# Memory-augmented attention kernel: adjacent score groups, halved second query/key chunk, memory sums in row tiles, last-token filler in column groups

## Chip, cores and metric

The kernel runs on one core of a Trainium2 chip. The metric is the device time of one execution in microseconds. Runs of the kernel before took 1844.02, 1857.45 and 1866.82 us; the median, 1857.45 us, is the time before. All profile times below come from one further execution under the profiler.

## What is computed

The program applies two block types twice: `x += A(ln(x))`, `x += B(ln(x))`, and both again. x is 2048 x 512 in bfloat16. B is a gated MLP with a spatial mix (w_sp, 2048 x 2048); the change does not touch it. A is attention with a memory that is carried from segment to segment, and only this part matters here:

```python
for s in range(n_seg):                       # 64 segments of 32 tokens
    h = concatenate([mem, xs])               # 8 memory rows + 32 tokens
    q, k, v = h @ Wq, h @ Wk, h @ Wv         # 32 heads of 128
    p = softmax(mask(q @ k.T * scale))
    o = (p @ v) @ Wo
    mem = o[:, :8]                           # feeds the next segment
    outs.append(o[:, 8:])
```

Segment s+1 cannot start its projections before segment s has produced its 8 new memory rows. So each attention block is a loop of 64 dependent segments, and there are 128 in the program.

## The kernel before, in words

**One segment.** `segment()` (L683) is a list of instructions in a fixed order: TensorE, VectorE and ScalarE run exactly in the order in which the program records them (`manual_schedule`, L511). GpSimd and the DMA queues are placed by the scheduler. The 40 rows of a segment are split. The 8 memory rows and the first 24 tokens are 32 rows that form `hA`, a 128x32 operand per quarter of the model dimension. The last 8 tokens of each of four segments are projected together for a block of 128 tokens (`hB`, 32 rows), one block ahead; that work is cut into small units and used as filler for TensorE (`b_units`, L570).

The segment's steps on TensorE, in order:

1. `qk(0)`, `qk(2)`, `qk(1)`, `qk(3)` (L762 to L767): q and k of the first and second half of the heads, called q0, k0, q1, k1 below. Each is one chunk of 16 matmuls, 32 columns of weights (hA) by 512 moving columns, in four column groups of the array, so that four run side by side (`mm_chunk`, L530). ScalarE casts the 128x512 result into `rows` (L701); VectorE turns it in 32x32 blocks into `QQ` or `KA` (L705).
2. `scores(0)` (L714): 16 pairs of keys and queries of the first half of the heads, in 64-column groups, into one bank of `psS`; then Exp on ScalarE (L726). `close(r)` (L728) multiplies by the mask on VectorE (L729).
3. `v_mm(0)`, a filler unit, `scores(1)`, `v_mm(1)`, a filler unit. The values are copied out by VectorE for half 0 (L776) and by ScalarE for half 1 (L782).
4. `psM` (L784 to L788): the softmax sums of the memory rows, four matmuls of the whole 128x128 array (`onesG` holds ones for one half of the partitions and zeros for the other), into the accumulator bank accB. ScalarE takes Ln and then Exp of -Ln (L802, L803): the reciprocal.
5. `pv(0)`, `pv(1)` (L739) and `psD`, the sums of the token rows (L793), in row tiles of 64. Then a filler unit.
6. VectorE multiplies the memory rows by the reciprocal (L807, one per half), and `wo_pass` (L595) multiplies all 32 heads by Wo: 128 matmuls of 128 columns in four column groups. Meanwhile ScalarE makes the reciprocals of the token rows (L805, L813), and `tok_out(0)` (L755) writes the first half's token rows: L757 for the first 24 tokens, L759 for the last 8.
7. `build_hA(s + 1)` (L651): copy_predicated puts the memory rows into the next segment's rows (L654), and a turn makes the next hA (L655). Then the output copy (L660), the fourth filler unit, `copies` (filler results, L586 on ScalarE), `tok_out(1)`, `turns` (filler results turned into the block's Q and K, L587 on VectorE), and `tail`.

**Filler.** Each segment has four filler points. In segments 1, 2 and 3 of a block they take `b_units`: two chunks of the next block's projection per segment, as 4, 4, 8 and 16 matmuls in column groups of 32; a result passes through the single bank accA. In the first segment of a block, from the fifth block on, they take `y_part` (L615): the last tokens' output projection, `wo_last` (L607), as 1, 1, 2 and 4 matmuls of the whole array, 512 columns each, summed by VectorE (L627). The first segments of the first four blocks and the last three segments of the last block have no filler. So the 128 segments are 90 with `b_units`, 24 with `y_part` and 14 with none.

**Pads.** `pads_of` (L671) splits some of the 512-column matmuls in two of 256, so that each segment has the same number of TensorE instructions, a whole number of pages of 256; `fills_of` (L663) gives the instructions of the four filler points. One matmul is two instructions, a weight load and the multiplication.

**PSUM.** Eight banks: accA and accB one each, `att` two (psS, later psD), `attO[0]` and `attO[1]` two each (values psV, later the PV results psO).

**Also running.** In some segments `spare1`, `spare2` and `tail` add row work to VectorE: residual add (L213), statistics (L138) and normalisation (L187, L223) of rows for the next stage.

Of the kernel before, what the change touches and what calls it, by code (L numbers as in the profile page):

```python
# [14 lines left out]
P = 128  # L15
# [463 lines left out]
def a_block(tc, c, rows, front, MV_in, RS_in, MV_out, RS_out, wqkv, Wo, S, first):  # L479
# [6 lines left out]
    with ExitStack() as ctx:  # L486
# [83 lines left out]
        def b_units(tb, early=False):  # L570
            bs = blk_state[tb]

            for k, j in enumerate((0, 2, 1, 3, 4, 5)):
                ps = (accA if k % 2 == 0 or not early else accB).tile([P, 512], F32, name="psb")
                for kts in (((0,), (1,), (2, 3)), ((0, 1, 2, 3),))[k % 2]:
                    mm_chunk(ps, lambda kt, cg: bs["hB"][:, kt, :],
                             lambda kt, cg: qk_rhs(j, kt, cg) if j < 4 else v_rhs(j - 4, kt, cg), kts)
                    if kts[-1] != KT - 1:
                        yield

                def out(j=j, ps=ps):
                    if j >= 4:
                        nc.scalar.copy(bs["VB"][:, j - 4].rearrange("p i e -> p (i e)"), ps[:])
                        return
                    r = rowp.tile([P, 512], BF16, name="rowsB", bufs=2)
                    nc.scalar.copy(r[:], ps[:])  # L586
# [17 lines left out]
        def store_last(G, eng):  # L604
            eng.dma_start(o_d[M + 512 * G:M + 512 * G + 512, :].rearrange("(j r) d -> j r d", r=32)[:, 24:32, :], yB.pop(G)[:])

        def wo_last(G, heads, pwB):  # L607

            for h in heads:
                n = h // 8 * 8 + 2 * (h % 4) + h // 4 % 2  # L610
                nc.tensor.matmul(pwB[:], lhsT=oBs[G][:, n, :], rhs=Wo_sb[:, h, :].rearrange("p (kt g el) -> p g kt el", kt=4, g=4),  # L611
                                 start=(h == heads[0]), stop=(h == heads[-1]))
                yield

        def y_part(G, q):  # L615

            pwB = accA.tile([P, DM], F32, name="pwB")
            for k, _ in enumerate(wo_last(G, range(8 * q, 8 * q + 8), pwB)):
# [12 lines left out]
            adds.append(out)  # L631
            yield
# [30 lines left out]
        def fills_of(s):  # L663

            if s < 0:
                return FILL_AHEAD[not first]
            if s % 4 == 0:
                return (2, 2, 4, 8) if s // 4 > 3 else (0, 0, 0, 0)
            return (8, 8, 16, 32) if s // 4 + 1 < NB else (0, 0, 0, 0)

        def pads_of(s):  # L671

            n = (3 * PE_PAGE - SEGMENT_PE - fills_of(s - 1)[3] - sum(fills_of(s)[:3]) + 1) // 2
            pads = dict.fromkeys(("q0", "k0", "q1", "k1", "v0", "v1"), 0)
            for chunk, most in (("v0", 16), ("k1", 16), ("v1", 16 if s % 4 == 0 else 8), ("q1", 12), ("k0", 8), ("q1", 16), ("v1", 16),
                                ("k0", 16), ("q0", 16)):
                k = min(n, most - pads[chunk])
                pads[chunk] += k
                n -= k
            assert n == 0  # L680
            return pads

        def segment(s, fill, spare1, spare2, tail):  # L683
# [20 lines left out]
            def qk_T(j, r):  # L704
                nc.vector.transpose(out=QQ[:, j % 2, :, 0:32] if j < 2 else KA[:, j % 2], in_=r[:])  # L705

            def v_mm(r, ps):
                mm_chunk(ps, lambda kt, cg: hA_cur[:, kt, :], lambda kt, cg: v_rhs(r, kt, cg), halved=pads[("v0", "v1")[r]])

# [4 lines left out]
            def scores(r):  # L714

                pS = psS[:, r, 0:448].rearrange("p (i c) -> p i c", i=4)
                for i in range(4):
                    for K, c0 in ((KA, 0), (KTB, 80)):
                        for g in range(2):
                            n = 4 * i + 2 * g  # L720
                            q = QQ[:, r, n:n + 2, :]
                            nc.tensor.matmul(pS[64 * g:64 * g + 64, i, c0:80 if K is KA else 112],  # L722
                                             lhsT=K[:, r, n:n + 2, :].rearrange("p h k -> p (h k)"),
                                             rhs=q if K is KA else ends(q),
                                             start=(i == 0 and K is KA), stop=True, tile_position=(0, 64 * g), skip_group_check=True)
                nc.scalar.activation(out=E[:, r], in_=pS, func=ACT.Exp, scale=scale)  # L726

            def close(r):  # L728
# [23 lines left out]
            def hview(t, r, lo, hi):  # L752
                return t.rearrange("p (b n) q -> p b n q", b=4)[:, 2 * r:2 * r + 2, :, lo:hi]

            def tok_out(r):  # L755
                Rr = Rt[:].rearrange("p g (r n q) -> p g r n q", r=2, n=8)[:, :, r]
                nc.vector.tensor_tensor(out=hview(uT_nxt[:], r, 8, 32), in0=oview(r, 8, 32),  # L757
                                        in1=Rr[:, :, :, 0:24], op=ALU.mult)
                nc.vector.tensor_tensor(out=hview(oB, r, 8 * (s % 16), 8 * (s % 16) + 8), in0=oview(r, 32, 40),  # L759
                                        in1=Rr[:, :, :, 24:32], op=ALU.mult)  # L760
# [24 lines left out]
            for g in range(2):  # L785
                o = psM[:, 128 * g:128 * g + 128]
                nc.tensor.matmul(o, lhsT=onesG[:, g, :], rhs=a_part(0, P, 0, 2, 0, 8), start=(g == 0), stop=True, skip_group_check=True)  # L787
                nc.tensor.matmul(o, lhsT=onesG[:, g, :], rhs=b_part(0, P, 0, 2, 0, 8), start=False, stop=True, skip_group_check=True)  # L788
            psO = [attO[r].tile([P, 2, 512], F32, name="psO") for r in range(2)]
            psD = att.tile([P, 2, 512], F32, name="psD")  # L790
            pv(0)
            pv(1)
            for part, q0, q1, c0 in ((a_part, 8, 40, 0), (b_part, 8, 16, 24)):  # L793
                for r in range(2):
                    for g in range(2):
                        o = psD[:, g, 256 * r:256 * r + 256].rearrange("p (n q) -> p n q", q=32)[:, :, c0:32]
                        nc.tensor.matmul(o, lhsT=ones[64 * g:64 * g + 64, :], rhs=part(64 * g, 64 * g + 64, r, r + 1, q0, q1),  # L797
                                         start=(part is a_part and r == 0), stop=True, skip_group_check=True)
# [3 lines left out]
            nc.scalar.activation(out=rm, in_=psM[:, 0:256], func=ACT.Ln)  # L802
            nc.scalar.activation(out=rm, in_=rm, func=ACT.Exp, scale=-1.0)  # L803
# [35 lines left out]
        for s in range(NSEG):  # L839
# [87 lines left out]
```

The softmax here doesn't subtract the row's maximum and nothing guards it: scores larger than these inputs give would overflow.

## Time and profile before

| what | value |
|---|---|
| median of 3 runs | 1857.45 us |
| profiled execution | 1850.3 us |
| its span, first to last instruction | 1848.6 us |
| granted TensorE clock, mean | 0.991 |
| first attention block, 52 to 773 us | 721 us; TensorE busy 706, VectorE 492, ScalarE 503 |
| first B block, 773 to 958 us | 185 us; TensorE busy 164 |
| second attention block, 958 to 1684 us | 726 us; TensorE busy 713, VectorE 486, ScalarE 503 |
| end, from 1684 us | 165 us |
| scores, matmuls (psS) | 4096, mean 184 to 208 ns each |
| psM, matmuls | 512, mean 219 and 223 ns |
| cast of a 128x512 chunk on ScalarE (L701) | 512 x 586 ns |
| turn of a 128x512 chunk on VectorE (L705) | 512 x 711 ns |
| Exp of the scores (L726) | 256 x 547 ns |
| mask product (L729) | 256 x 372 ns |
| Ln, Exp for the memory rows (L802, L803) | 128 x 385 ns, 128 x 417 ns |

A matmul's duration is from its issue to its end; matmuls are pipelined, so that successive ones start much closer together than they last. How much time a stretch costs is therefore read from starts, not from sums of durations.

### The profile page before, as it was taken

How to read it: one execution, taken by the hardware profiler on the slowest of the kernel's cores; microseconds unless marked ns; L12 is line 12 of the kernel's file. 1: busy time of each engine (PE TensorE's matmuls, PEld its weight loads, DVE VectorE, ACT ScalarE, POOL GpSimd, SP SyncE). 2: the span in 40 equal slices, each digit the busy share in tenths (PEclk: the TensorE clock that was granted, in tenths of full speed). 3: DMA queues.
4: the chain of work that ended last, by engine and by line, in shares of the span. 5: the costliest groups of instructions: out<-in, count | busy, mean ns of one | idle time of the engine just before them, and what ended most of it. 6: DMA issues, size and time to landing. Idle time of an engine off the chain costs nothing.

```text
span 1848.6 us, 109448 instructions
## 1 busy us (share of the span) xinstructions
PE 1749.7 (95%) x51152; PEld 1246.7 (67%) x51176; DVE 1155.0 (62%) x2700; ACT 1111.5 (60%) x2074; POOL 137.1 (7%) x289
## 2 busy tenths in 40 slices
PE   2999999999999999889989999999999999998898
PEld 1777777777777777645547777777777777775455
DVE  1666666677667766584346666666766676665622
ACT  1667777767777766471036667677776777665500
POOL 5000000000000000032010000000000000003000
PEclk8999999999999999999999999999999999999999
DMA  9100000021002111268940000001200121125585
GB/s 347 54 20 19 20 20 21 21 71 41 20 20 82 35 30 34 88 157 172 201 134 22 23 22 22 22 22 45 82 25 23 48 86 26 35 62 150 113 174 131
DMA packets 189327, 126.78 MB, mean 69 GB/s; under 512 B 135896, under 2 KB 164328, under 8 KB 188872
## 3 DMA queue, kind: packets, MB, share of 16 engines
q1 hardware_dynamic: 167016, 71.01, 16.6%
q0 software_dynamic: 10560, 34.07, 5.6%
q10 hardware_dynamic: 11296, 14.70, 2.7%
q8 instruction: 400, 6.55, 1.5%
q14 instruction: 55, 0.45, 0.1%
HBM read 59.29 MB, written 33.56 MB: 50 GB/s over the span
## 4 chain that ended last, share of the span: by engine, by line
PE 86%; DMA 4%; DVE 4%; issue 3%; ACT 2%; POOL 1%; SPq 0%; ACTq 0%; POOLq 0%; DVEq 0%
PE psm L544 24%; PE psV L544 13%; PE pw L599 12%; PE psb L544 10%; PE pg L332 7%; PE psS L722 5%; PE psO L745 4%; PE pwB L611 3%; PE py L360 2%; PE psD L797 2%; PE pz L266 1%; PE psM L787 1%; DMA uT<-u 1%; DMA Wo_sb<-in_A_Wo_dram 1%; PE psM L788 1%
## 5 line engine op out<-in xcount | busy, mean ns | idle before, releaser
L544 PEld LDWEIGHTS <-hA 128*32 128x32 bf16 x19868 | 542.2, 96 | 167.7 <-DVE hA L655 51.6
L701 ACT CAST rows<-psm 128x512 bf16<-128x512 f32 x512 | 300.2, 586 | 197.8 <-PE psm L544 197.8
L544 PE MATMUL psm<-Wq_sb,hA 128*32 128x256 bf16 (+1 forms) x5768 | 274.4, 319 | 11.2 <-DVE hA L655 9.5
L599 PEld LDWEIGHTS <-uT 128*32 128x32 bf16 x16640 | 236.1, 97 | 59.9 <-DVE uT L807 49.8
L599 PE MATMUL pw<-Wo_sb,uT 128*32 128x128 bf16 x16640 | 262.5, 220 | 14.6 <-DVE uT L807 6.3
L544 PE MATMUL psm<-Wk_sb,hA 128*32 128x256 bf16 (+1 forms) x6623 | 275.0, 298 | 1.4 <-issue 0.7
L544 PE MATMUL psV<-Wv_sb,hA 128*32 128x256 bf16 x7477 | 274.7, 284 | 1.1 <-issue 1.0
L705 DVE STREAM_TRANSPOSE QQ<-rows 128x512 bf16<-128x512 bf16 x256 | 182.0, 711 | 77.9 <-ACT rows L701 76.7
L726 ACT ACTIVATE E<-psS 128x448 bf16<-128x448 f32 x256 | 140.0, 547 | 121.8 <-PE psS L722 121.8
L757 DVE TENSOR_TENSOR uT<-psO,Rt 128x384 bf16<-128x384 f32 x256 | 138.6, 541 | 119.3 <-ACT Rt L813 119.0
L705 DVE STREAM_TRANSPOSE KA<-rows 128x512 bf16<-128x512 bf16 x256 | 181.7, 710 | 43.5 <-ACT rows L701 43.2
L807 DVE TENSOR_TENSOR uT<-psO,Rm 128x128 bf16<-128x128 f32 x256 | 62.5, 286 | 169.5 <-PE psD L797 169.5
L813 ACT ACTIVATE Rt<-Rt 128x512 f32<-128x512 f32 x256 | 157.4, 629 | 4.1
L332 PE MATMUL pg<-z2n,wspT 128*128 128x344 bf16 x1024 | 156.1, 311 | 1.0 <-DVE u L340 1.0
L332 PEld LDWEIGHTS <-wspT 128*128 128x128 bf16 x1024 | 98.4, 98 | 55.4 <-issue 8.2
L805 ACT ACTIVATE Rt<-psD 128x1024 f32<-128x1024 f32 x128 | 131.2, 1025 | 6.0
L544 PEld LDWEIGHTS <-hB 128*32 128x32 bf16 x3072 | 88.4, 97 | 68.4 <-DVE hB L559 25.2
L722 PEld LDWEIGHTS <-KA 128*64 128x64 bf16 x2048 | 79.8, 113 | 67.1 <-DVE KA L705 40.4
L729 DVE TENSOR_TENSOR E<-E,maskN 128x448 bf16<-128x448 bf16 x256 | 95.2, 372 | 45.7 <-ACT E L726 45.7
L544 PE MATMUL psb<-Wq_sb,hB 128*32 128x512 bf16 x1024 | 92.1, 390 | 26.2 <-DVE hB L559 26.2
L782 ACT CAST VA<-psV 128x512 bf16<-128x512 f32 x128 | 75.0, 586 | 62.7 <-PE psV L544 62.7
L722 PE MATMUL psS<-QQ,KA 128*64 128x80 bf16 x2048 | 110.1, 208 | 1.9 <-issue 0.9
(147 smaller groups left out, 2219.4 us busy)
## 6 DMA issues: line engine op xcount, KB each, us to landing
Wo_sb<-in_A_Wo_dram POOLq DMA_DIRECT2D x8, 1024.0 KB, 13.5
xs<-xd ACTq DMA_DIRECT2D x32, 256.0 KB
o_d<-o_sb SPq DMA_DIRECT2D x126, 64.0 KB
y_o<-o_d SPq DMA_DIRECT2D x24, 256.0 KB
xd<-y_o SPq DMA_DIRECT2D x22, 256.0 KB
Wq_sb<-in_A_Wq_dram POOLq DMA_DIRECT2D x8, 512.0 KB, 7.2
Wk_sb<-in_A_Wk_dram POOLq DMA_DIRECT2D x8, 512.0 KB, 11.1
Wv_sb<-in_A_Wv_dram POOLq DMA_DIRECT2D x8, 512.0 KB, 11.5
```

The source lines that it names most:

```text
L332: nc.tensor.matmul(pg[t][:, k, 0:344], lhsT=wsp[t][:, st, :], rhs=z2n[:, st, 344 * k:344 * k + 344], start=(st == 0), stop=(st == NT - 1))
L544: nc.tensor.matmul(o, lhsT=lhs(kt, cg), rhs=r, start=(kt == 0 and a == 0), stop=(kt == KT - 1 or halved > 0), tile_position=(0, 32 * cg), ...
L599: nc.tensor.matmul(po[32 * cg:32 * cg + 32, 0:128], lhsT=lhs[:, n, :], rhs=wo_rhs(h, cg), start=(h == 0), stop=(h == H - 1), tile_position ...
L701: nc.scalar.copy(r[:], ps[:])
L705: nc.vector.transpose(out=QQ[:, j % 2, :, 0:32] if j < 2 else KA[:, j % 2], in_=r[:])
L722: nc.tensor.matmul(pS[64 * g:64 * g + 64, i, c0:80 if K is KA else 112], lhsT=K[:, r, n:n + 2, :].rearrange("p h k -> p (h k)"), rhs=q if ...
L726: nc.scalar.activation(out=E[:, r], in_=pS, func=ACT.Exp, scale=scale)
L729: nc.vector.tensor_tensor(out=E[:, r], in0=E[:, r], in1=maskN[:, j4, :].unsqueeze(1).to_broadcast([P, 4, 112]), op=ALU.mult)
L757: nc.vector.tensor_tensor(out=hview(uT_nxt[:], r, 8, 32), in0=oview(r, 8, 32), in1=Rr[:, :, :, 0:24], op=ALU.mult)
L782: nc.scalar.copy(VA[:, 1].rearrange("p i e -> p (i e)"), psV[1][:, 0, :])
L805: nc.scalar.activation(out=Rt[:], in_=psD[:], func=ACT.Ln)
L813: nc.scalar.activation(out=rt, in_=rt, func=ACT.Exp, scale=-1.0)
```

## The change

Six edits, nearly all in `segment()`:

- **Second chunk in halves.** q1 and k1 are computed by `qk_halves`: two passes of 16 matmuls with 256 columns, each pass into a bank of its own in `attO`; ScalarE casts and VectorE turns each half by itself. The four turns become two of 128x512 and four of 128x256.
- **Both score groups adjacent.** The order is now q0, k0, q1, k1, v0, scores 0, scores 1, v1, two filler units, psM. Both Exps are recorded after both groups, both mask products after both Exps. v1 goes through accB.
- **Memory sums in PV's tiling.** psM multiplies 64 partitions at a time with plain ones, as PV and psD do, and its two halves lie in two banks of `attO[1]`. The second PV, which needs `attO[1]`, follows psD and the Ln that reads psM; the third filler unit follows it.
- **Last-token product later.** The part of `tok_out` that writes the last 8 tokens becomes `last_out`; for half 0 it stands behind `build_hA`.
- **Last-token filler in column groups.** `wo_last` with `parts=4` splits each matmul of the whole array into four with 32 weight columns, side by side. The final pass at the end of the block keeps the whole array.
- **Filler bank.** Every second chunk of `b_units` (except in the early pass) goes into `att` instead of accA.

`fills_of` and `pads_of` follow: the number of TensorE instructions of a segment stays.

```diff
             for k, j in enumerate((0, 2, 1, 3, 4, 5)):
-                ps = (accA if k % 2 == 0 or not early else accB).tile([P, 512], F32, name="psb")
+                if early or k % 2 == 0:
+                    ps = (accA if k % 2 == 0 else accB).tile([P, 512], F32, name="psb")[:]
+                else:
+                    ps = att.tile([P, 2, 512], F32, name="psb2")[:, 0, :]
...
-        def wo_last(G, heads, pwB):
+        def wo_last(G, heads, pwB, parts=1):
+            w = P // parts
             for h in heads:
                 n = h // 8 * 8 + 2 * (h % 4) + h // 4 % 2
-                nc.tensor.matmul(pwB[:], lhsT=oBs[G][:, n, :], rhs=Wo_sb[:, h, :].rearrange("p (kt g el) -> p g kt el", kt=4, g=4),
-                                 start=(h == heads[0]), stop=(h == heads[-1]))
+                for t in range(0, P, w):
+                    nc.tensor.matmul(pwB[t:t + w, :], lhsT=oBs[G][:, n, t:t + w], rhs=Wo_sb[:, h, :].rearrange("p (kt g el) -> p g kt el", kt=4, g=4),
+                                     start=(h == heads[0]), stop=(h == heads[-1]), tile_position=(0, t))
                 yield
...
-                return (2, 2, 4, 8) if s // 4 > 3 else (0, 0, 0, 0)
+                return (8, 8, 16, 32) if s // 4 > 3 else (0, 0, 0, 0)
...
-            pads = dict.fromkeys(("q0", "k0", "q1", "k1", "v0", "v1"), 0)
-            for chunk, most in (("v0", 16), ("k1", 16), ("v1", 16 if s % 4 == 0 else 8), ("q1", 12), ("k0", 8), ("q1", 16), ("v1", 16),
-                                ("k0", 16), ("q0", 16)):
+            pads = dict(q0=0, k0=0, q1=16, k1=16, v0=0, v1=0)
+            n -= 32
+            for chunk, most in (("k0", 8), ("v0", 8), ("v1", 8), ("v0", 16), ("k0", 16), ("v1", 16), ("q0", 16)):
...
+            def qk_halves(j):
+                ps = attO[j // 2].tile([P, 2, 512], F32, name="psm2")
+                r = rowp.tile([P, 512], BF16, name="rows", tag="rowsQK", bufs=4)
+                for a in range(2):
+                    for kt in range(KT):
+                        for cg in range(4):
+                            nc.tensor.matmul(ps[32 * cg:32 * cg + 32, a, 0:256].rearrange("p (i c) -> p i c", i=2), lhsT=hA_cur[:, kt, :],
+                                             rhs=qk_rhs(j, kt, cg)[:, 2 * a:2 * a + 2], start=(kt == 0), stop=(kt == KT - 1),
+                                             tile_position=(0, 32 * cg))
+                    nc.scalar.copy(r[:, 256 * a:256 * a + 256], ps[:, a, 0:256])
+                    yield
+                    out = (QQ[:, 1, :, 0:32] if j < 2 else KA[:, 1])[:, 8 * a:8 * a + 8]
+                    nc.vector.transpose(out=out, in_=r[:, 256 * a:256 * a + 256])
...
             r0 = qk(0)
             r2 = qk(2)
             qk_T(0, r0)
-            r1 = qk(1)
             qk_T(2, r2)
-            r3 = qk(3)
-            qk_T(1, r1)
+            q1, k1 = qk_halves(1), qk_halves(3)
+            for g in (q1, q1, k1, q1, k1, k1):
+                next(g, None)
+            psV = attO[0].tile([P, 2, 512], F32, name="psV")
+            v_mm(0, psV[:, 0, :])
+            nc.vector.tensor_copy(VA[:, 0].rearrange("p i e -> p (i e)"), psV[:, 0, :])
             psS = att.tile([P, 2, 512], F32, name="psS")
-            scores(0)
-            qk_T(3, r3)
-            psV = [attO[r].tile([P, 2, 512], F32, name="psV") for r in range(2)]
-            v_mm(0, psV[0][:, 0, :])
+            pS = [scores(r) for r in range(2)]
+            for r in range(2):
+                exps(r, pS[r])
+            for r in range(2):
+                close(r)
+            spare1()
+            psW = accB.tile([P, 512], F32, name="psV")
+            v_mm(1, psW)
             fill()
-            close(0)
-            nc.vector.tensor_copy(VA[:, 0].rearrange("p i e -> p (i e)"), psV[0][:, 0, :])
-            scores(1)
-            close(1)
-            spare1()
-            v_mm(1, psV[1][:, 0, :])
             fill()
-            nc.scalar.copy(VA[:, 1].rearrange("p i e -> p (i e)"), psV[1][:, 0, :])
-            psM = accB.tile([P, 512], F32, name="psM")
-            for g in range(2):
-                o = psM[:, 128 * g:128 * g + 128]
-                nc.tensor.matmul(o, lhsT=onesG[:, g, :], rhs=a_part(0, P, 0, 2, 0, 8), start=(g == 0), stop=True, skip_group_check=True)
-                nc.tensor.matmul(o, lhsT=onesG[:, g, :], rhs=b_part(0, P, 0, 2, 0, 8), start=False, stop=True, skip_group_check=True)
-            psO = [attO[r].tile([P, 2, 512], F32, name="psO") for r in range(2)]
+            nc.scalar.copy(VA[:, 1].rearrange("p i e -> p (i e)"), psW[:])
+            psM = attO[1].tile([P, 2, 512], F32, name="psM")
+            for part in (a_part, b_part):
+                for g in range(2):
+                    nc.tensor.matmul(psM[:, g, 0:128], lhsT=ones[64 * g:64 * g + 64, :], rhs=part(64 * g, 64 * g + 64, 0, 2, 0, 8),
+                                     start=(part is a_part), stop=True, skip_group_check=True)
+            psO = [attO[0].tile([P, 2, 512], F32, name="psO")]
             psD = att.tile([P, 2, 512], F32, name="psD")
             pv(0)
-            pv(1)
...
+            Rm = segp.tile([P, 2, 2, 64], F32, name="Rm", bufs=1)
+            rm = Rm[:].rearrange("p g r c -> p g (r c)")
+            nc.scalar.activation(out=rm, in_=psM[:, :, 0:128], func=ACT.Ln)
+            nc.scalar.activation(out=rm, in_=rm, func=ACT.Exp, scale=-1.0)
+            psO.append(attO[1].tile([P, 2, 512], F32, name="psO"))
+            pv(1)
             fill()
-            Rm = segp.tile([P, 2, 2, 64], F32, name="Rm", bufs=1)
-            rm = Rm[:].rearrange("p g r c -> p (g r c)")
-            nc.scalar.activation(out=rm, in_=psM[:, 0:256], func=ACT.Ln)
-            nc.scalar.activation(out=rm, in_=rm, func=ACT.Exp, scale=-1.0)
...
             tok_out(0)
             if s + 1 < NSEG:
                 build_hA(s + 1, pw)
+            last_out(0)
             if s > 0:
                 store_o(s, pw, nc.sync)
             fill()
             run(copies)
             run(adds)
             tok_out(1)
+            last_out(1)
             run(turns)
             tail()
```

More of the change, by code (lines that the diff above doesn't have):

```diff
@@ L582, in out @@
                     if j >= 4:
-                        nc.scalar.copy(bs["VB"][:, j - 4].rearrange("p i e -> p (i e)"), ps[:])
+                        nc.scalar.copy(bs["VB"][:, j - 4].rearrange("p i e -> p (i e)"), ps)
                         return
                     r = rowp.tile([P, 512], BF16, name="rowsB", bufs=2)
-                    nc.scalar.copy(r[:], ps[:])
+                    nc.scalar.copy(r[:], ps)
                     turns.append(lambda: nc.vector.transpose(
@@ L617, in y_part @@
             pwB = accA.tile([P, DM], F32, name="pwB")
-            for k, _ in enumerate(wo_last(G, range(8 * q, 8 * q + 8), pwB)):
+            for k, _ in enumerate(wo_last(G, range(8 * q, 8 * q + 8), pwB, 4)):
                 if k in (0, 1, 3):
@@ L725, in scores, with exps @@
                                              start=(i == 0 and K is KA), stop=True, tile_position=(0, 64 * g), skip_group_check=True)
+                return pS
+            def exps(r, pS):
                 nc.scalar.activation(out=E[:, r], in_=pS, func=ACT.Exp, scale=scale)
@@ L753, in hview, with r_view, last_out @@
                 return t.rearrange("p (b n) q -> p b n q", b=4)[:, 2 * r:2 * r + 2, :, lo:hi]
+            def r_view(r):
+                return Rt[:].rearrange("p g (r n q) -> p g r n q", r=2, n=8)[:, :, r]
             def tok_out(r):
-                Rr = Rt[:].rearrange("p g (r n q) -> p g r n q", r=2, n=8)[:, :, r]
                 nc.vector.tensor_tensor(out=hview(uT_nxt[:], r, 8, 32), in0=oview(r, 8, 32),
-                                        in1=Rr[:, :, :, 0:24], op=ALU.mult)
+                                        in1=r_view(r)[:, :, :, 0:24], op=ALU.mult)
+            def last_out(r):
                 nc.vector.tensor_tensor(out=hview(oB, r, 8 * (s % 16), 8 * (s % 16) + 8), in0=oview(r, 32, 40),
-                                        in1=Rr[:, :, :, 24:32], op=ALU.mult)
+                                        in1=r_view(r)[:, :, :, 24:32], op=ALU.mult)
             r0 = qk(0)
```

## The prediction

> **What bounds the kernel now.** I read the page's engine totals and its chain first:
>
> ```profile
> PE 1749.7 (95%) x51152; PEld 1246.7 (67%) x51176; DVE 1155.0 (62%) x2700; ACT 1111.5 (60%) x2074; POOL 137.1 (7%) x289
> ...
> PE 86%; DMA 4%; DVE 4%; issue 3%; ACT 2%; POOL 1%; SPq 0%; ACTq 0%; POOLq 0%; DVEq 0%
> ```
>
> TensorE is busy 95% of the span and holds 86% of the chain. The busy-by-stretch view puts 721 us (52 to 773) and 726 us (958 to 1684) into the two attention blocks. These are 128 segments that run one after the other, since each needs the memory rows of the one before. So I read one segment in the chain of waits, us 304.7 to 316.1 (start, length, what):
>
> ```profile
> 304.92 3.49 PE psm L544 x88
> 308.41 0.38 PE psS L722 x16
> 308.79 1.00 PE psV L544 x32
> 309.78 0.21 PE psb L544 x4
> 310.00 0.38 PE psS L722 x16
> 310.37 0.99 PE psV L544 x16
> ...
> 313.33 1.80 PE pw L599 x128
> ```
>
> It looks like pure TensorE work. The timeline of the same place shows a second chain just as tight:
>
> ```profile
> 304.06 0.28 DVE L654 CAST_PREDICATED pre<-maskM,pw 128x128 bf16<-128x128 uint16 x1
> 304.37 0.31 DVE L655 STREAM_TRANSPOSE hA<-pre 128x128 bf16<-128x128 bf16 x1
> 304.74 3.39 PEld L544 LDWEIGHTS <-hA 128*32 128x32 bf16 x92 [0.31 <-DVE hA L655]
> ...
> 310.42 0.55 ACT L726 ACTIVATE E<-psS 128x448 bf16<-128x448 f32 x1 [0.92 <-PE psS L722]
> 311.00 0.39 DVE L729 TENSOR_TENSOR E<-E,maskN 128x448 bf16<-128x448 bf16 x1 [0.32 <-ACT E L726]
> 311.18 0.40 PE L544 MATMUL psb<-Wv_sb,hB 128*32 128x512 bf16 x4
> 311.51 0.23 PE L787 MATMUL psM<-E,onesG 128*128 128x128 bf16 x1
> 311.95 0.38 ACT L802 ACTIVATE Rm<-psM 128x256 f32<-128x256 f32 x1
> 312.36 0.42 ACT L803 ACTIVATE Rm<-Rm 128x256 f32<-128x256 f32 x1
> 312.71 0.62 PE L544 MATMUL psb<-Wv_sb,hB 128*32 128x512 bf16 x8
> 312.81 0.49 DVE L807 TENSOR_TENSOR uT<-psO,Rm 128x128 bf16<-128x128 f32 x2 [1.42 <-PE psD L797]
> 313.15 1.80 PEld L599 LDWEIGHTS <-uT 128*32 128x32 bf16 x128 [0.32 <-DVE uT L807]
> ```
>
> hA is turned by 304.68 and q0 starts at 304.74: no slack. psM, Ln, Exp and the first of the two L807 (0.29 each on the page) end about 313.10, and the Wo pass loads its weights at 313.15 and starts at 313.16: no slack either. Only from q0 to psM is TensorE alone the limit: the mask product ends at 311.39, psM starts at 311.51. So a segment with next-block projections as filler ("b segment") is q0 to psM 6.77 (304.74 to 311.51), psM to Wo 1.65 (to 313.16), Wo to the next q0 2.74 (to 315.90), together 11.16. The next one, with last-token Wo filler ("y segment"), takes 11.50 (315.90 to 327.40).
>
> **What the skill says.** The Trainium skill, TensorEngine Tiling (Array Packing), Key Properties: a change of tiling mode, not of tile, drains TensorE. The trace agrees: four psb matmuls take 0.22 where the mode stays (eight from 312.71 to Wo's 313.16) and 0.33 where psM follows (311.18 to 311.51), so a switch is about 0.10. PSUM — Partial Sum Buffer, PSUM bank collisions: two engines may not touch one bank in one quadrant at once; hence halves and sums get banks of their own, and the second PV must wait until Ln has read psM. No run here shows a collision. TensorE: Matmul & The Clock Gate, What overlaps: matmuls keep strict order, so whatever waits at psM holds all behind it. VectorE: DVE Perf Modes, The TRN2 errata: a fixed cost per instruction and about a cycle per element; the trace agrees (128x128 turn 0.31, 128x512 turn 0.71).
>
> **The change, part by part.**
>
> *TensorE alone, b segment.* Today seven mode switches: into the first scores, out, into the second, out, into psM (whole array), into PV, out. After: into the scores, out, into the row tiles of psM/PV/psD, out. Three fewer: 0.29. psM is four matmuls some 0.056 apart (0.06 in the chain); in PV's row tiles two and two overlap: 0.11 less. The fourth filler waited 0.07 for the copy that frees accA (the pass is 1.80 in the chain, but in the timeline the filler starts 1.88 after it, at 303.88, with the copy L586 ending 303.83); its own bank removes that. Halving q1 and k1 fully costs about 0.02; the total of TensorE instructions per segment is kept. On TensorE alone: some 0.47 less. But the other chain does not shrink by as much.
>
> *q0 to psM, after.* q0, k0, q1, k1 take 3.60 less the switch that no longer follows, 3.50; v0 0.87 and a switch: scores start at 4.48. Two groups of eight steps, 0.035 each in the timeline: last score starts 5.03, ends 5.22. In the built program's order the first Exp carries the wait for TensorE and the second carries none: both hang on the last score of group two. Exp 5.26; the second 0.44 later (0.547 less 0.10, by which ACT's neighbours overlap: a cast from 308.47 takes 0.59, the Exp after it starts 308.95), done 6.25; mask 6.28 to 6.67; psM 6.73 (0.055 from VectorE to TensorE, as at hA). TensorE would be there at 5.14 + 0.87 + 2 x 0.22 + 0.11 = 6.57. So a new wait of 0.16 stands at psM, and against today's 6.77 only 0.04 is gained. Queued behind it: PV, sums, filler, Wo.
>
> *psM to Wo.* First to last psM start 0.07 instead of 0.18. From the last one the chain stays (0.22 end, Ln 0.38, Exp 0.42, L807 0.29, hand-overs: 1.47). Wo at 8.27: 1.54 instead of 1.65. The second PV waits for Ln to 7.48 (TensorE ready 7.37); filler then ends at 8.28, so this new wait costs 0.01, hidden by the Exp and L807; without that cover 0.11.
>
> *Wo to q0.* The last-token product (0.20 of VectorE's time) goes behind hA; L654 started about 0.04 late for it. 2.70 instead of 2.74; the removed 0.07 at accA lies under this chain and is worth nothing.
>
> Sum 6.73 + 1.54 + 2.70 = 10.97: 0.19 less in each of 90 b segments, 17.1 us.
>
> *y segment.* Eleven switches become four, and Wo filler has the b filler's shape: on TensorE alone it becomes a b segment, so it lands on the same chain, plus about 0.05 because k0 needs accA after yB's add (L627, about 0.69 after the filler's end): 11.02 instead of 11.50, 0.48 x 24 = 11.5 us.
>
> *Fourteen segments without filler* were bound by the second chain already; I take 0.05 each: 0.7 us.
>
> *VectorE.* Four half turns instead of two whole ones. No row shows a 128x256 turn: between 0.31 and 0.71 I take 0.44 (the errata page's form gives an estimate of 0.42); ends are 0.31 (nothing gained, since ACT's copies pace it) and 0.71 (a rival below). Pitch 0.37, as neighbours overlap by 0.08 (L655 ends 304.68, the next starts 304.61). k0's turn starts 2.58; the halves follow, the last waiting for its copy at 4.31 and ending 4.75; the scores need it at 4.91. Half copies on ACT: between Ln's 0.38 (128x256) and below; 0.37. But where VectorE still has two rowsB turns and a row norm (L223, 0.5) in front, now 0.20 later too, the last half ends near 5.15 and the scores stall about 0.25. Of the 24 row norms two in three stand behind two turns (the third chunk pair is values, with none): 16 x 0.25 = 4.0 us lost. The SP and POOL queues keep their DMAs; the QQ copy waits for scores as before.
>
> Total 17.1 + 11.5 + 0.7 - 4.0 = 25.3 us of the span's 1848.6 (the profiled execution took 1850.3): 1823.3, or 1.37%. The median shown, 1857.45, is 0.4% above the profiled execution; in its terms 1857.45 x 0.9863 = 1832.
>
> **Rivals.** *TensorE stays the only bound* (the softmax chain proves shorter): if Exp overlaps the second group after all, psM comes at 6.57, a b segment at 10.81 (-0.35), a y segment at 10.86 (-0.64): 31.5 + 15.4 + 0.7 = 48 us, 1800 in profile, 1809 in the median's terms. For it: 95% busy TensorE. Against: the single wait of both Exps.
>
> *New waits take it all back*: the second score group stalls 0.25 in every b segment, not in 16, and y segments gain half: 90 x (0.25 - 0.19) = 5 us lost, 6 gained: about 1856. For it: VectorE is then in one unbroken row of turns from k0's to the last half. Against: a slack of 0.16 in the ordinary segment.
>
> *Slower*: one mechanism, the half turn's price at L725. If a half costs as much as a whole, pitch 0.63, the last ends at 2.58 + 0.63 + 4 x 0.63 + 0.08 = 5.81, where the scores want it at 4.91: 0.95 of stall less 0.19 in 114 segments, some 80 us, 1940. It decides against the change by 2% (37 us, 0.33 a segment) once the last half ends 0.52 late, a half turn of 0.60. Against: the 128x128 turn at 0.31.
>
> *It does not do what it says*: switches might not vanish, if column groups of the Wo filler cost more than psb's. Then y stays at 11.5: 1844.
>
> **How the numbers follow.** My forecast 0.50, its own range 1820 to 1845. TensorE the only bound 0.20. Waits take it back 0.14, no y gain 0.06. Slower 0.10. About 2% (37 us) is what a measurement of this kernel can tell from no change. Faster by over 2%: the first rival and a tail of the forecast, 0.23. Slower by over 2%: 0.10. Within: 0.67. The range reaches from the first rival's 1809, less 9 for the spread of runs (1844 to 1867), to the waits' 1856 plus 9: 1800 to 1865.
>
> **What would show it.** Right: b segments at 10.9 to 11.0, psM's release by the mask product with TensorE idle 0.1 to 0.2 before it; both Exps back to back after the last score; a wait before the second PV on Ln of about 0.1; y segments like b segments; half turns near 0.44. Wrong: Exp starting before group two ends; a b segment under 10.85; score matmuls waiting for L725 in ordinary segments; TensorE idle at q0 for something other than hA.

## The result, and the profile after

The changed kernel takes 1977.22 us (median of four runs, 1975.68 to 1978.83) beside 1859.4 us for the kernel before on the same chip. The ratio is 1.064, interval 1.058 to 1.071: slower by 6.4%, outside the predicted range of 1800 to 1865. The profiled execution has a span of 1975.0 us at a granted clock of 0.989 (before: 1848.6 at 0.991), so the clock is not the reason.

The page of the changed kernel, its engine totals, its chain and the groups of two new lines, L722 and L719 (the last column is the idle time of the engine just ahead of them, and what ended it):

```profile
PE 1747.0 (88%) x51178; PEld 1268.6 (64%) x51178; DVE 1215.3 (62%) x2956; ACT 1132.0 (57%) x2330; POOL 136.9 (7%) x289
...
PE 71%; ACT 15%; DVE 6%; issue 4%; DMA 3%; POOL 0%; SPq 0%; ACTq 0%; POOLq 0%; DVEq 0%
...
L722 ACT CAST rows<-psm 128x256 bf16<-128x256 f32 x512 | 191.3, 374 | 192.0 <-PE psm L719 183.8
...
L719 PE MATMUL psm<-Wq_sb,hA 128*32 128x256 bf16 x4096 | 160.7, 273 | 67.7 <-ACT rows L722 67.7
L719 PE MATMUL psm<-Wk_sb,hA 128*32 128x256 bf16 x4096 | 159.2, 273 | 60.2 <-ACT rows L722 60.2
```

TensorE does the same amount of work, 1747 us busy, in a longer span, and ScalarE's share of the chain goes from 2% to 15%. The two groups of L719, the halved q1 and k1, show why: TensorE stands ahead of them for ScalarE's cast of `rows` (L722), and that cast in turn stands for them. The two engines take turns. Such a stand of TensorE is called a hold below. The timeline of one segment shows how (start, length, engine, what, idle before it and what ended that):

```profile
328.48 1.05 PE L544 MATMUL psm<-Wq_sb,hA 128*32 128x512 bf16 x16
329.35 1.05 PE L544 MATMUL psm<-Wk_sb,hA 128*32 128x512 bf16 x24
...
330.22 0.62 PE L719 MATMUL psm<-Wq_sb,hA 128*32 128x256 bf16 x16
...
330.94 0.38 ACT L722 CAST rows<-psm 128x256 bf16<-128x256 f32 x1
331.37 0.62 PE L719 MATMUL psm<-Wq_sb,hA 128*32 128x256 bf16 x16 [0.53 <-ACT rows L722]
331.80 0.62 PE L719 MATMUL psm<-Wk_sb,hA 128*32 128x256 bf16 x16
332.04 0.81 ACT L722 CAST rows<-psm 128x256 bf16<-128x256 f32 x2 [0.72 <-PE psm L719]
332.90 0.62 PE L719 MATMUL psm<-Wk_sb,hA 128*32 128x256 bf16 x16 [0.47 <-ACT rows L722]
333.33 0.61 PE L544 MATMUL psV<-Wv_sb,hA 128*32 128x512 bf16 x10
```

The second half of q1 starts 0.05 after the cast of the first half ends (331.32), and the second half of k1 likewise waits for k1's first cast. A half that is not held takes 0.43 from its start to the next start (331.37 to 331.80); the held ones come after 1.15 and 1.10. The halves do go to different banks, `ps[:, 0]` and `ps[:, 1]`, but the change takes both banks as one tile (`psm2`, 128 x 2 x 512), and in this program a write to a tile whose other bank is being read still waits for that reader: in the trace, the first matmul of each second half carries a wait that the cast ends. So q0 to v0 takes 4.85 (328.48 to 333.33), where I had 3.50. Everything behind it is on time, as the timeline of the same segment shows:

```profile
335.08 0.98 ACT L749 ACTIVATE E<-psS 128x448 bf16<-128x448 f32 x2 [1.14 <-PE psS L742]
335.65 0.83 DVE L752 TENSOR_TENSOR E<-E,maskN 128x448 bf16<-128x448 bf16 x2 [0.52 <-ACT E L749]
...
336.53 0.29 PE L815 MATMUL psM<-E,ones 64*128 64x128 bf16 x4
...
336.86 0.39 ACT L828 ACTIVATE Rm<-psM 128x256 f32<-128x256 f32 x1 [0.20 <-PE psM L815]
337.27 0.42 ACT L829 ACTIVATE Rm<-Rm 128x256 f32<-128x256 f32 x1
337.29 0.21 PE L768 MATMUL psO<-E,VA 64*128 64x80 bf16 x2
...
337.72 0.49 DVE L836 TENSOR_TENSOR uT<-psO,Rm 128x128 bf16<-128x128 f32 x2 [1.24 <-PE psO L768]
```

psM starts 8.05 after q0 (forecast 6.73, plus 1.35 of holds), Wo at 338.07 is 1.54 after psM (forecast 1.54), the next q0 at 340.78 is 2.71 after Wo (forecast 2.70). From one Wo start to the next, 57 of the 90 b segments take 12.30 to 12.31 and 21 of the 24 y segments 12.35 to 12.36; the rest are longer.

### The profile page after: what moved, and what is told of

The parts are those of the page before. It is cut to its first block, busy times and chain, and to the rows that moved or that the text cites. A ratio compares the mean times of both kernels' runs of the same rounds, so it can differ in the third digit from the quotient of the medians.

```text
span 1975.0 us, 109986 instructions
## 1 busy us (share of the span) xinstructions
PE 1747.0 (88%) x51178; PEld 1268.6 (64%) x51178; DVE 1215.3 (62%) x2956; ACT 1132.0 (57%) x2330; POOL 136.9 (7%) x289
## 4 chain that ended last, share of the span: by engine, by line
PE 71%; ACT 15%; DVE 6%; issue 4%; DMA 3%; POOL 0%; SPq 0%; ACTq 0%; POOLq 0%; DVEq 0%
PE psm L544 12%; PE pw L602 11%; PE psm L719 11%; PE pg L332 7%; PE psb L544 7%; ACT E L749 6%; PE psV L544 6%; ACT rows L722 4%; PE psS L742 4%; PE psO L768 4%; ACT rows L706 4%; DVE E L752 3%; PE py L360 2%; PE pwB L616 2%; PE psM L815 2%
## 5 line engine op out<-in xcount | busy, mean ns | idle before, releaser
L544 PEld LDWEIGHTS <-hA 128*32 128x32 bf16 x11102 | 354.0, 96 | 136.7 <-DVE hA L660 54.7
L719 PEld LDWEIGHTS <-hA 128*32 128x32 bf16 x8192 | 232.4, 96 | 180.7 <-issue 180.1
L722 ACT CAST rows<-psm 128x256 bf16<-128x256 f32 x512 | 191.3, 374 | 192.0 <-PE psm L719 183.8
L544 PE MATMUL psV<-Wv_sb,hA 128*32 128x512 bf16 (+1 forms) x5880 | 271.1, 315 | 0.0
L706 ACT CAST rows<-psm 128x512 bf16<-128x512 f32 x256 | 150.1, 586 | 124.8 <-PE psm L544 124.8
L719 PE MATMUL psm<-Wq_sb,hA 128*32 128x256 bf16 x4096 | 160.7, 273 | 67.7 <-ACT rows L722 67.7
L719 PE MATMUL psm<-Wk_sb,hA 128*32 128x256 bf16 x4096 | 159.2, 273 | 60.2 <-ACT rows L722 60.2
L725 DVE STREAM_TRANSPOSE KA<-rows 128x256 bf16<-128x256 bf16 x256 | 114.0, 446 | 82.5 <-ACT rows L722 82.5
L544 PE MATMUL psm<-Wq_sb,hA 128*32 128x512 bf16 x2064 | 135.6, 383 | 10.5 <-DVE hA L660 8.9
L544 PE MATMUL psm<-Wk_sb,hA 128*32 128x256 bf16 (+1 forms) x3158 | 140.2, 306 | 1.9 <-issue 1.4
L725 DVE STREAM_TRANSPOSE QQ<-rows 128x256 bf16<-128x256 bf16 x256 | 108.5, 424 | 38.6 <-ACT rows L722 38.5
L544 PEld LDWEIGHTS <-hB 128*32 128x32 bf16 x3072 | 79.3, 98 | 67.4 <-DVE hB L559 24.7
```

Source lines behind the costliest of these rows:

```text
L544: nc.tensor.matmul(o, lhsT=lhs(kt, cg), rhs=r, start=(kt == 0 and a == 0), stop=(kt == KT - 1 or halved > 0), tile_position=(0, 32 * cg), ...
L719: nc.tensor.matmul(ps[32 * cg:32 * cg + 32, a, 0:256].rearrange("p (i c) -> p i c", i=2), lhsT=hA_cur[:, kt, :], rhs=qk_rhs(j, kt, cg)[:, ...
L722: nc.scalar.copy(r[:, 256 * a:256 * a + 256], ps[:, a, 0:256])
L725: nc.vector.transpose(out=out, in_=r[:, 256 * a:256 * a + 256])
```

## Experiments

A segment's time is given from its Wo start to the next in the trace, unless another start is named. "Undisturbed" is the shortest time that recurs in many segments of a kind; others are longer by some late piece. In the changed kernel most b segments are undisturbed, in runs 1, 5 and 6 only 12 to 20 of 126 segments. "e5" in an expectation is run 5. Runs 1 to 4, 5 to 8 and 9 to 10 were made on three chips, on which the kernel before took 1841.91, 1851.43 and 1848.67 us; so runs of different groups are compared by their ratios.

**1. The halves in four tiles.** q1's halves go to `attO[0]` and `attO[1]`, k1's to accB and `att`, each a tile by itself. The rest of the change stays.

```diff
+            def half_bank(j, a):
+                if j // 2 == 0:
+                    return attO[a].tile([P, 2, 512], F32, name="psm2")[:, 0, :]
+                return accB.tile([P, 512], F32, name="psm3")[:] if a == 0 else att.tile([P, 2, 512], F32, name="psm4")[:, 0, :]
...
-                ps = attO[j // 2].tile([P, 2, 512], F32, name="psm2")
...
                 for a in range(2):
+                    ps = half_bank(j, a)
...
```

> The kernel after, but the four halves of q1 and k1 go to four PSUM tiles (attO[0], attO[1], accB, att) in place of two. Theory T (the second half of each chunk is held until ScalarE has cast the first, because both are one tile): the two holds of about 0.67 us each vanish from all 128 segments, a filler segment falls from 12.30 to about 10.96, the run from 1977 to 1800-1830, below the kernel before. Rival R1 (four casts and four turns are too slow for ScalarE and VectorE, whoever owns the banks): the stall moves to the scores, 1850 or more. Rival R2 (two passes of 256 columns are slow on TensorE itself, weight loads idle 180 us): q1 and k1 stay at 1.5 each, about 1970.

Measured: 1884.37 us, ratio 1.022 (1.020 to 1.025). The holds are gone: no matmul of the halves (L724 here) stands for their cast (L727) any more. The timeline of one segment:

```profile
332.86 1.05 PE L544 MATMUL psm<-Wq_sb,hA 128*32 128x512 bf16 x16
333.74 1.05 PE L544 MATMUL psm<-Wk_sb,hA 128*32 128x512 bf16 x24
334.60 1.06 PE L724 MATMUL psm<-Wq_sb,hA 128*32 128x256 bf16 x32
335.47 1.06 PE L724 MATMUL psm<-Wk_sb,hA 128*32 128x256 bf16 x32
336.35 1.06 PE L544 MATMUL psV<-Wv_sb,hA 128*32 128x512 bf16 x24
```

q0 to v0 is 3.49, and an undisturbed segment is 10.93 to 10.94, close to my sum, which had no holds (10.97). But the total missed its expectation by more than 50 us: in the second attention block hardly a segment is undisturbed; nine in ten take 11.4 to 12.8. That opened a second question, taken up from run 5 on.

**2. Whole chunks.** The change with `qk(1)` and `qk(3)` again, one cast and one turn of 512 columns each: all but the halving. (The pads still split their matmuls in two of 256 columns, and their tiles are accB and accA again.)

```diff
-            q1, k1 = qk_halves(1), qk_halves(3)
-            for g in (q1, q1, k1, q1, k1, k1):
-                next(g, None)
+            r1 = qk(1)
+            qk_T(1, r1)
+            r3 = qk(3)
+            qk_T(3, r3)
```

> The kernel after, but q1 and k1 are whole chunks again, with cast and turn of 512 columns as before; the scores stay adjacent and all other edits stay. T: no hold at the halves; the second score group waits about 0.35 for the one long turn of k1, segment about 11.3, run 1845-1870. R1: faster than e1. R2: as fast as e1.

Measured: 1853.35 us, ratio 1.006 (1.004 to 1.008), segments of 11.32. The second score group starts 0.38 after the last pair of the first group has started, instead of 0.03 (334.25 to 334.63), held by the long turn of k1. So the halving has a use, 0.4 a segment, if nothing holds it. Without it the rest of the change does not pay: a b segment took 11.16 before.

**3. The kernel before with nothing but the halves**, in one tile as in the change (and the change's pads).

```diff
...
-            r1 = qk(1)
             qk_T(2, r2)
-            r3 = qk(3)
-            qk_T(1, r1)
+            q1, k1 = qk_halves(1), qk_halves(3)
+            for g in (q1, q1, k1, q1, k1):
+                next(g, None)
             psS = att.tile([P, 2, 512], F32, name="psS")
             scores(0)
-            qk_T(3, r3)
+            next(k1, None)
```

> The kernel before with one part of the change alone: q1 and k1 in halves, two halves in one tile; scores, sums, fillers and everything else as before. T: the holds come back at full price, since TensorE keeps its order: 1.2 to 1.4 us per segment, 2010-2035. A rival that blames the adjacent scores or the row-tiled sums for the loss expects 1850-1870 here.

Measured: 2001.29 us, ratio 1.086 (1.084 to 1.089); segments 12.52, q0 to the scores 4.97 instead of 3.60. The view of the waits on TensorE (total, times, longest) has almost the same row in the changed kernel and here:

```profile
PE psm L719 <- ACT rows L722: 127.9, 256, 0.5
...
PE psm L714 <- ACT rows L717: 127.7, 256, 0.6
```

The halves in one tile alone bring the whole loss, 1.37 a segment from q0 to the scores. With run 1 this settles the cause of the result from both sides.

**4. The kernel before with the last-token filler in column groups**, nothing else.

```diff
-                nc.tensor.matmul(pwB[:], lhsT=oBs[G][:, n, :], rhs=...)
+                for t in range(0, P, w):
+                    nc.tensor.matmul(pwB[t:t + w, :], lhsT=oBs[G][:, n, t:t + w], rhs=..., tile_position=(0, t))
...
+            for k, _ in enumerate(wo_last(G, range(8 * q, 8 * q + 8), pwB, 4)):
...
-                return (2, 2, 4, 8) if s // 4 > 3 else (0, 0, 0, 0)
+                return (8, 8, 16, 32) if s // 4 > 3 else (0, 0, 0, 0)
```

> The kernel before with the last-token filler in four column groups alone. If mode switches cost 0.10 each and four of the eleven of such a segment go: 24 x 0.35 = 8 us less, 1845-1853. If the switches cost nothing or the column groups cost as much: no change.

Measured: 1834.59 us, ratio 0.995 (0.993 to 0.997). From q0 to q0, the y segments go from 11.50 to 11.16, the time of a b segment. The mode switches at the ends of the fillers were the whole of their difference. Within the longest filler unit, the time from the first start to the last is 0.658 in both shapes. What changes lies at the ends: the first unit starts 0.09 instead of 0.21 after the matmul ahead of it, and Wo starts 0.21 instead of 0.31 after the last matmul of the third unit.

**Where run 1 lost its gain.** Its timeline in the second attention block, around the end of a Wo pass and the filler behind it:

```profile
1171.00 1.51 PE L602 MATMUL pw<-Wo_sb,uT 128*32 128x128 bf16 x96
1172.34 0.81 PE L544 MATMUL psb<-Wk_sb,hB 128*32 128x512 bf16 x9
1174.02 0.61 PE L544 MATMUL psb<-Wk_sb,hB 128*32 128x512 bf16 x7 [0.87 <-issue]
```

TensorE stops within a filler chunk for 0.87, and waits for nothing that the profile shows. Such pauses come every 767 to 769 recorded TensorE instructions. Section 3 of the page has a candidate, the queue of instruction packets:

```profile
q8 instruction: 400, 6.55, 1.4%
```

The trace has these 400 packets at 16,384 bytes each, and it records 102,495 TensorE instructions; 400 times 256 is 102,400. The Trainium skill, Perfetto Trace Analysis, The 4-stage abstract model, says that an instruction has 64 bytes; 16,384 bytes are then 256 instructions, and the trace's count agrees. So I take this to be TensorE's program, fetched in pages of 256, and `pads_of` keeps a segment at 768 = 3 pages so that the page ends stay at the same places in every segment. In run 1 the score tile came into the bank of k1's second half, which needed one more wait instruction on TensorE per segment: 769. (The trace of run 1 has 160 such instructions of TensorE, that of the changed kernel 32: one more in each of the 128 segments.) The page ends crept through the segment by one instruction each time. By that place (number of the instruction at which the Wo pass ends, modulo 256, counted from the program's start), the mean segment of run 1 was longer than 10.94 by:

| place | 94 to 101 | 102 to 109 | 110 to 117 | 118 to 133 | 134 to 149 | 150 to 157 | 158 to 173 | 174 to 221 |
|---|---|---|---|---|---|---|---|---|
| extra, us | 0.10 | 0.05 | 0.17 | 0.39 | 0.65 | 0.81 | 0.97 | 1.2 |

In the pause shown, the last packet before it starts at 1171.67 and TensorE goes on at 1174.02, 2.35 later.

**5. 768 again.** Run 1 with k1's second half in accA, so that the additional wait instruction disappears (the trace has 32 again); the place is 93 throughout.

```diff
...
-                return accB.tile([P, 512], F32, name="psm3")[:] if a == 0 else att.tile([P, 2, 512], F32, name="psm4")[:, 0, :]
+                return (accB, accA)[a].tile([P, 512], F32, name=("psm3", "psm4")[a])[:]
```

> Run one missed its time because a segment had 769 TensorE instructions instead of 768: its last score tile stood in the bank of k1's second half, which cost one more wait instruction per segment. 769 is three pages of 256 and one, so the place of the page ends creeps through the segment by one instruction each time (Wo pass ends at 94 of a page in segment 0, at 158 in segment 64, at 221 in the last), and in the second half TensorE stands once per segment for 0.7 to 1.3 us with nothing to wait for but its instructions. Here k1's second half goes to the bank of k0 instead, nothing else differs, and every segment has 768 again. Page theory: every segment 10.94 (90 x 0.22 + 24 x 0.56 + 14 x 0.1 = 35 us below before), no idle 'issue' pauses beyond those of before (about 30 us of the 1884 gone at least), 1805 to 1825 where before has 1842 to 1859. Rival, the extra time of run one comes from late rows or transfers because segments are faster: segments of 11.5 to 12.3 stay in the second half, 1870 to 1890.

Measured: 1838.76 us, ratio 0.993 (0.991 to 0.996). Faster than before by 0.7%, and by 3% faster than run 1, but not the 1805 to 1825 expected. Idle time on "issue" (a wait for nothing that the profile shows) ahead of TensorE's matmuls, summed over the rows of the waits, falls from 65.0 in run 1 to 21.3; the spans of these two executions differ by 39.2. The kernel before has 8.6. Weight loads show it too: those of L544 and of the Wo pass stand 67.5 on "issue" here, 35.9 before. Median segment 11.23, fastest 10.93. It seems that the denser segment runs into the pages at places that cost the kernel before little.

**6. Score groups in two tiles.** Run 5, with the second group in `attO[1]`.

```diff
...
-            psS = att.tile([P, 2, 512], F32, name="psS")
+            psS = [(att, attO[1])[r].tile([P, 2, 512], F32, name="psS") for r in range(2)]
...
```

> As the run before (four tiles for the halves, 768 instructions), and the two score groups in tiles of their own, so that the first Exp waits for group one alone and not for group two. If the new wait at psM (0.13 to 0.16 a segment) comes from the two Exps starting together, the b segment falls from 10.94 to 10.80 to 10.83 and the whole by 14 to 18 us; if psM is then held by the second group's mask product all the same (Exp 0.54, mask 0.39 after group two), it stays within 3 us.

Measured: 1830.94 us, ratio 0.989 (0.987 to 0.992); undisturbed segments 10.79, though the median is 11.22. The timeline around psM:

```profile
642.30 0.98 ACT L754 ACTIVATE E<-psS 128x448 bf16<-128x448 f32 x2 [0.88 <-PE psS L747]
642.34 0.19 PE L747 MATMUL psS<-QQ,old 128*64 128x32 bf16 x2
...
642.87 0.83 DVE L757 TENSOR_TENSOR E<-E,maskN 128x448 bf16<-128x448 bf16 x2 [0.25 <-ACT E L754]
...
643.88 0.29 PE L820 MATMUL psM<-E,ones 64*128 64x128 bf16 x4
```

Exp now starts before the last score does; in the changed kernel it starts 0.04 after the last score's end. The mask product ends 0.18 before psM, where in the changed kernel it ended 0.05 before. The wait at psM is gone, 0.14 in an undisturbed segment, as expected; of the 14 to 18 us, 8 were measured, and the intervals of runs 5 and 6 meet.

**7. Run 5 with the page ends elsewhere.** 48 matmuls (96 instructions) once, ahead of the first q0: place 189 instead of 93. Every segment keeps its instructions and waits.

```diff
+                for _ in range(48 if first and s == 0 and j == 0 else 0):
+                    nc.tensor.matmul(ps[0:32, 0:128], lhsT=hA_cur[:, 0, :], rhs=Wq_sb[:, 0, 0:128], start=True, stop=True, tile_position=(0, 0))
```

> e5 with 48 more matmuls (96 instructions) once, ahead of the first q0: the work of a segment, its 768 instructions and its waits stay, only the page ends lie 96 instructions earlier in it (Wo pass ends at 189 of a page instead of 93). Page theory: a pause of 0.9 to 1.3 us in the fillers after Wo in every segment, as run one had in the segments with this place, so 12.0 to 12.2 a segment and 115 to 155 us above e5. Rival (place of no matter): 5 us above e5, the cost of the 48 matmuls.

Measured (two executions): 1920.32 us, ratio 1.037 (1.034 to 1.041): 82 us over run 5, where place of no matter would give 5. Its waits on TensorE have rows that run 5 lacks:

```profile
PE psb L544 <- issue: 67.4, 90, 1.4
...
PE pwB L616 <- issue: 21.0, 26, 1.8
```

One pause in the filler in each of the 90 b segments. All "issue" ahead of matmuls: 91.2, which is 69.9 more than in run 5; the span is 69.1 longer. The pauses are shorter than expected (0.75 against 0.9 to 1.3), so the lower end of 115 us was not reached.

**8. The kernel before with the same 96 instructions** (place 186 instead of 90).

> The kernel before with the same 96 instructions once at its start (Wo pass ends at 186 of a page instead of 90). If the pause belongs to the place of the page end and not to the change, its segments of 11.16 become 12.0 to 12.4 and the time rises by 100 to 150 us; if only the changed kernel's denser fillers can outrun the fetch, it stays within 10 us.

Measured (two executions): 1907.17 us, ratio 1.030 (1.027 to 1.033), 56 us more. "Issue" ahead of matmuls goes from 8.6 to 56.8, with the same row for 90 pauses:

```profile
PE psb L544 <- issue: 49.1, 90, 1.6
```

The page ends matter for either kernel; the sum was half of what I had expected. The y segments, whose filler is of the whole array here, kept their time (11.59 in the median from q0 to q0, before 11.52).

**9 and 10. Run 6 with 12 and with 20 instructions ahead**: places 105 and 113.

> e6 with 6 more matmuls (12 instructions) once ahead of the first q0, so that the Wo pass ends at 105 of a page of 256 instructions instead of 93. In run one, whose place crept from 94 to 221, the mean extra of a segment over its undisturbed 10.94 was 0.05 at 102 to 109, 0.10 at 94 to 101, 0.17 at 110 to 117, 0.4 at 118 to 133 and 1.2 to 1.3 from 174 on; e6, at 93, stands 0.1 to 0.3 us at page ends in the Wo pass, in k0 and in v1. Page theory: the extras of e6 (about 0.3 a segment) fall to about 0.1, 20 to 25 us, so 1805 to 1815 against 1831. Rival, those extras are late rows: within 4 us of e6.

> The same with 10 more matmuls (20 instructions): the Wo pass ends at 113 of a page. By run one's table 0.1 a segment more than at 105, so 10 to 15 us above it and 5 to 15 below e6. Rival (place of no matter at this scale): the same as e6 and e9 within 4 us.

Measured: 1822.63 us, ratio 0.987 (0.984 to 0.990), and 1831.17, ratio 0.991 (0.988 to 0.993). Place 105 has the lowest time of all, 1.3% under the kernel before, but the gain on run 6 is within the intervals and far from the 20 to 25 us expected. "Issue" ahead of matmuls is 24.2 and 20.6 beside 21.5 in run 6: the pauses only went elsewhere, from Wo and k0 to k0 and the scores. Run 1's table, taken at segments of 10.94, does not carry over at this scale.

The traces tell more directly that the stalls of these runs sit at page ends. Take every step from one matmul's start to the next in the two attention blocks, leaving out those that end another wait than "issue". Compare it with the usual step between the same two kinds (their lower quartile), and add up the excess wherever it is over 0.1. Sorted by the number of the recorded TensorE instruction, modulo 256, the numbers 192 to 195 stand out in each of runs 5 to 10, in this order: 59, 67, 135, 89, 53 and 57 us, and at most 27 us in any other four. In the changed kernel it is 13. The segment was moved against the pages in runs 7 to 10, and the stalls stayed with the pages. Places 186 and 189 put the end of the Wo pass just ahead of these numbers, and so the page end into the filler behind it. So late rows are not what these 53 to 135 us are made of.

## Why the prediction was wrong

**The step that failed: "q0, k0, q1, k1 take 3.60 less the switch that no longer follows, 3.50".** Measured 4.85. I had read "each pass into a bank of its own", and from the Trainium skill, PSUM — Partial Sum Buffer, PSUM bank collisions, I went on to "hence halves and sums get banks of their own", as if the bank decided who waits. The program's waits go by tile: the first matmul of the second half carries a wait for L722, which I had put at nothing; of the built program's waits I had followed those of the Exps alone. The cost is 0.72 + 0.67 a segment, the two delays beyond 0.43 (1.36 when q0 to v0 is compared with run 1's 3.49). Runs 1 and 3 show that it is this and nothing else in an undisturbed segment: without it 10.94 where 10.97 was forecast, with it alone 1.37 more.

**The sum.** 90 b segments at 12.30 instead of 10.97 are 120 us, 24 y segments at 12.35 instead of 11.02 are 32: the 152 by which the span (1975.0) passes my 1823.3. That it fits so closely is partly chance, for it takes every segment at its usual length and leaves out those without filler. By the means from q0 to q0, b segments went from 11.28 to 12.35, y segments from 11.60 to 12.45, and the 12 without filler that can be measured so from 12.22 to 12.81: together 124 of the 126.4 by which the span grew. Two sums of the prediction are slightly off: the parts of the 0.47 on TensorE give 0.45, and the stall of 0.95 in *Slower* is 0.90 (5.81 less 4.91). Neither moves the forecast.

**Steps that held.** Rest of the b segment: 0.14 at psM (forecast 0.16), both Exps after group two, psM to Wo 1.54, Wo to q0 2.71. The second PV starts at 337.29, right after Ln (337.25). The y segment is a b segment and 0.05, as forecast (12.35 beside 12.30). Half turns took 0.42 to 0.45 on L725 and 0.40 where nothing holds the casts (forecast 0.44), half casts 0.37. The Wo filler: run 4 gives the 0.34 per y segment. The three fewer switches of a b segment have no run of their own; run 6's 10.79 agrees with the 10.81 that counts them.

**Steps that did not show.** The 4.0 us for row norms ahead of the last turn: in the changed kernel the scores start 0.98 to 0.99 after v0 in all 128 segments, since the holds give the turns 1.35 more. In run 5, scores wait for the turns 26.0 us in 121 places, 0.21 each, an ordinary hand-over in nearly every segment (before: 40.4 in 135), not 16 stalls of 0.25.

**The rivals.** *Slower* was given 0.10, for the price of a half turn; that price was right, and the slowness came from TensorE's wait for the cast, a path that I had not opened. *TensorE the only bound* (10.81 a segment) is what run 6 shows where it is undisturbed: 10.79. It still did not give that rival's 48 us but 20; the 67 us of stalls at page ends in run 6 are more than enough for the rest. "The total of TensorE instructions per segment is kept" was all that I had said on pages. It was true of the change (its "issue" ahead of matmuls is 5.2), but it said nothing of how much room a faster segment leaves for the fetch. That a faster segment has less of it is argued, not tested by itself: run 5 and the kernel before stand at nearly the same place, 93 and 90, with 21.3 and 8.6 on "issue".

**Left open.** What sets the moment at which a page is asked for: between the start of the last packet and the end of a pause over 0.4, TensorE ran 84 to 213 recorded instructions in the median of a run, and from none to 265 in single cases. So I cannot say which place would be best, only that 93, 105 and 113 are within 9 us of each other and that 186 and 189 cost 56 and 82.

## What to carry to other kernels

Before counting a split as free overlap, look up for each new piece which wait its first instruction carries: two banks in one tile are one object to the waits, and a tile per piece gave back the whole 1.35 a segment here. When TensorE's program is long and dense, count its instructions per round of the loop: one additional wait instruction moved the page ends on by one each round, and the run with it was 39 us of span longer than the run without it, more than the change could gain. And after a stall is removed, expect the next limit close behind; here 10.94, then 10.79, then the fetch.

## What the hardware showed beside that

After a pause at a page end TensorE mostly went on 2.3 to 2.7 us after the start of the last packet before it (2.35 at 1174.02 in run 1, 2.62 at 304.76 in run 7, 2.36 at 634.83 in run 6), in runs 5, 6, 9 and 10 often later, in all up to 3.5, though a packet itself takes 0.9 to 1.5, seldom up to 1.9. A Wo pass of 256 instructions takes 1.80, which is less. Ninety-six more instructions, once, at the start of the kernel before, of which the trace records 102,365 on TensorE, made it 3.0% slower.
